# A Fourier mixing and MLP-Mixer kernel: seven-product form in three more chunks, an earlier front for batch 1, and a token relu in halves

## The chip, the cores and the metric

The kernel runs on one core of a Trainium2 chip. The metric is the device time in microseconds of one execution. The engines named below are TensorE (PE, matmuls; PEld is its weight load), VectorE (DVE), ScalarE (ACT), GpSimd (POOL) and SyncE (SP, which here only issues DMAs). Matmuls write to PSUM; DVE and ACT move their results from there to SBUF.

## What is computed

```python
def _attn_ref(x):                       # x: (8, 3008, 256) float32
    X = np.fft.fft(x, axis=1)
    X = np.fft.fft(X, axis=2)
    return X.real.astype(np.float32)

def _moe_ref(x, w_tok1, w_tok2, w_ch1, w_ch2):
    xt = x.transpose(0, 2, 1)
    h = np.maximum(xt @ w_tok1, 0.0) @ w_tok2      # tokens: 3008 -> 256 -> 3008
    u = x + h.transpose(0, 2, 1)
    h2 = np.maximum(u @ w_ch1, 0.0) @ w_ch2        # channels: 256 -> 1536 -> 256
    return (u + h2).astype(np.float32)

def reference(x, moe_w_tok1, moe_w_tok2, moe_w_ch1, moe_w_ch2):
    return _moe_ref(_attn_ref(x), moe_w_tok1, moe_w_tok2, moe_w_ch1, moe_w_ch2)
```

Eight batches go through the same steps. The output is 8 x 3008 x 256 in float32.

## The kernel before

**Stages of one batch.** A batch goes through three stages.

- *fold* (`fold`, lines 321 to 343): the loaded x (two tiles, xp and xm) is added to its mirror image into eo, in 17 steps of a generator. Batches 0 and 1 are folded on DVE, later ones on POOL.
- *front* (`front`, lines 414 to 550): a generator whose every `yield` ends one step. Eight steps make z (a small matmul pz with the fold's result, then a copy out of PSUM), twelve make w (pw, which reads all of z), then come the token product `tok1` (pt, with the carried weights hp and hq, a difference and a sum, and a relu into uu), `y` (py, a copy sqy, then yt) and `tok2` (pu, added to yt into ut, in twelve steps). For batches after the first this is 45 steps in all. `rot` fills one column of w.
- *channel MLP*: ut is cut into 6 chunks of 512 columns (the sixth has 448). `mm1` makes for each chunk the twelve products pc and evicts each with a relu into c1[:, ct]; `mm2` or `mm2_seven` multiplies c1 by wc2, adds the transposed ut (uT, brought by a DMA transpose on SP) and stores the result.

**Two forms of the second product.** `mm2` (line 668) runs four stores ks, each of 12 matmuls with 256 columns. `mm2_seven` (line 633) computes the same 2 by 2 block product with seven block products instead of eight: seven times 12 matmuls with 128 columns, with four sums of c1's quarters (`sums`, s1 to s4), partly summed weights t1w to t4w and b22 (made once on POOL by `weight_sums`) and seven small additions on DVE. `seven(b, c)` says which chunks use which form. The sixth chunk has only 448 columns; for an even batch its last 64 are put aside in tail1, and the following odd batch's sixth chunk gets them in its columns 448 to 511, so that this chunk is full.

**What sets the order.** The order on each engine is the order in which the program issues, written out by hand. The main loop (line 751) runs over batches, chunks c and ct, and slot = 12 c + ct. In each slot it issues one pc of this chunk, then a part of the previous chunk's second product (`places` and `sum_at` say at which ct, or every third ct for `mm2`), then parts of other batches: for batch 0 what is left of its own front (`own_at`), the fold of batch 1 and the copy w2r of the token weights on POOL; then, from slot `first` on, steps of the next batch's front, NFRONT of them spread evenly up to slot 71; and at the slots of `fold_at` parts of the fold after next, on POOL, each behind a small copy `hold` that ties them to a sum s4.

**Buffers.** PSUM has three buffers "mm" for pc, three "f" for the front's products and two for the second product. A new pc waits until an earlier one has been evicted. c1 has two buffers.

**Who evicts.** In `mm1` ct 0, 3, 6 and 9 are evicted by DVE and the others by ACT; where the previous chunk uses `mm2_seven`, ACT does all (`joins`). z copies of half 0 go to DVE and of half 1 to ACT for batches after the first, except for the last two small ones, which both go to DVE (line 442).

**Lines to recognize in the profile.** L90 is the helper `tt` (all two-input operations), L84 `ts`, L97 `act` (all of ACT), L101 `copy`. L424, L433 and L438 are pz, L448 and L450 pw, L517 pt, L474 py, L495 pu, L576 pc, L626 the seven products, L681 `mm2`.

Of the kernel before, what the change touches and what calls it, by code (L numbers as in the profile page):

```python
# [36 lines left out]
def kernel(  # L37
# [31 lines left out]
    def ps_f(name, dt=FP32, n=512):  # L69
        return psum.tile([P, n], dt, tag="f", name=name, bufs=3)  # L70
# [28 lines left out]
    def copy(e, out_, in_):  # L99
        if e:  # L100
            V.tensor_copy(out=out_, in_=in_)  # L101
        else:
            act(out_, in_)
# [310 lines left out]
    def front(b):  # L414
# [15 lines left out]
        for half in range(2):  # L430
            c = slice(half * P, (half + 1) * P)
            pz = ps_f("pz")
            nc.tensor.matmul(pz[:, 0:24], lhsT=eo[:, 0, c], rhs=t1n[:, half, 0, :],  # L433
                             start=True, stop=half == 0)
            if half:
                nc.tensor.matmul(pz[:, 0:24], lhsT=e128[:], rhs=cms[:],
                                 start=False, stop=True)
            nc.tensor.matmul(pz[:, 24:96], lhsT=eo[:, 16, c],  # L438
                             rhs=t1b[:].rearrange("p a k -> p (a k)"),
                             start=True, stop=True)  # L440
            zo = z[:, half, :, :].rearrange("p k (u s) -> p u k s", u=4)[:, :, :, 0]
            copy(b > 0 or half, zo, pz[:, 0:96].rearrange("p (u k) -> p u k", u=4))
            yield
        w = perb.tile([P, NG, 257], FP16, tag="w", name="w", bufs=2)
        zg = z[:].rearrange("p h (g i) s -> p h g (i s)", i=2)
# [65 lines left out]
        def tok1():  # L511
            for th in range(2):
                c = slice(th * P, (th + 1) * P)
                pt = ps_f("pt1")
                for o, n, w0, hw in ((0, 129, 0, hp), (129, 127, 130, hq)):
                    for g in range(NG):
                        nc.tensor.matmul(pt[:, o:o + n], lhsT=hw[:, g, c],  # L517
                                         rhs=w[:, g, w0:w0 + n],
                                         start=(g == 0), stop=(g == NG - 1))
                sq = perb.tile([P, P], FP32, tag="squ", name="squ", bufs=2)  # L520
                act(sq[:], pt[:, P:2 * P])
                uv = perb.tile([P, 2, P], FP32, tag="uv", name="uv", bufs=2)
                tt(uv[:, 0, :], pt[:, 0:P], sq[:], AT.subtract)
                tt(uv[:, 1, :], pt[:, 0:P], sq[:], AT.add)
                ts(uu[:, th, :, :], uv[:], 0.0, AT.max)
                yield
                if th == 0 and b > 0:
                    yield from rot()
# [25 lines left out]
                               for n in ("b22", "t1w", "t2w", "t3w", "t4w"))  # L554

    def seven(b, c):
        return c < NCH - 1 and (b > 0 or c >= 2)

    def weight_sums():
        G.tensor_copy(out=wc2[:, :, D:D + 1], in_=wc2[:, :, P:P + 1])  # L560
# [5 lines left out]
        tt(t3w[:], b22[:], b12, AT.subtract, G)  # L566
        tt(t4w[:], hi[:, :, 0:P], t2w[:], AT.subtract, G)

    def mm1(b, c, c1, ct, joins, cts=None):
        ut = state[b]["ut"]  # L570
        n = min(CW, S - CW * c)
        cts = cts or (ct,)
        pcs = [ps_mm("pc") for _ in cts]
        for h in range(2):
            for pc, ct in zip(pcs, cts):
                nc.tensor.matmul(pc[:, 0:n], lhsT=wc1[:, h, ct * P:(ct + 1) * P],  # L576
                                 rhs=ut[:, c, h, 0:n], start=(h == 0), stop=(h == 1))
# [125 lines left out]
    def take(g, n):  # L703
        for _ in range(n):
            next(g, None)
# [45 lines left out]
    for b in range(BB):  # L751
        nxt = front(b + 1) if b + 1 < BB else iter(())
        fold1 = fold(1, V) if b == 0 and BB > 1 else iter(())
        first, done = (31 if b == 0 else 0), 0
        for c in range(NCH):
            fold_at = {42: 5, 54: 5, 66: 7} if b == 0 else {30: 4, 42: 4, 54: 4, 66: 5}
            c1 = work.tile([P, NCT, CW], FP16, tag="c1", name="c1", bufs=2)
            box = {}
            joins = prev is not None and seven(*prev[0:2])
            for ct in range(NCT):  # L760
                slot = NCT * c + ct
                if b == 0 and slot < 3:
                    if slot == 0:
                        mm1(b, c, c1, ct, joins, range(3))
                else:
                    mm1(b, c, c1, ct, joins)
# [4 lines left out]
                if prev is not None and seven(*prev[0:2]):  # L771
                    if ct in places:
                        mm2_seven(*prev, places[ct], pbox)
                    if ct in sum_at:
                        sums(prev[2], pbox, sum_at[ct])
                elif prev is not None and ct % 3 == 2:
                    mm2(*prev, ct // 3, pbox)
                if slot == 1 and b == 0:
                    weight_sums()
                if b == 0:  # L780
                    take(own, own_at.get(slot, 0))
                    if 10 <= slot < 27:
                        take(fold1, 1)
                    if slot == 27 and BB > 2:
                        load_x(2)
                    if slot in (27, 29, 31, 33):
                        th, hb = (slot - 27) // 4, (slot - 27) // 2 % 2
                        G.tensor_copy(out=w2r[:, th, 32 * hb:32 * hb + 32, 0:NQ],
                                      in_=w2v[0][:, th, 32 * hb:32 * hb + 32, :])
                while done < NFRONT * (slot + 1 - first) // (71 - first):  # L790
                    take(nxt, 1)
                    done += 1
                if slot in fold_at:
                    if b + 2 < BB:
                        if slot == min(fold_at):
                            fold2 = fold(b + 2, G)
                        G.tensor_copy(out=hold[:], in_=pbox[4][:, 0, 0, 0:1])  # L797
                        take(fold2, fold_at[slot])
                    if slot == max(fold_at) and b + 3 < BB:
                        load_x(b + 3)  # L800
            if c == 5:
                if b % 2:
                    G.tensor_copy(out=c1[:, :, 448:512], in_=tail1[:])
                else:
                    G.tensor_copy(out=tail1[:], in_=c1[:, :, 384:448])
            prev, pbox, uT = (b, c, c1, uT), box, uT_next
    for s in range(4):
        mm2(*prev, s, pbox)
# [30 lines left out]
```

## Time and profile before

| what | value |
|---|---|
| time, three runs | 609.38 us median (608.84 to 610.14) |
| the profiled execution | 609.21 us |
| its span, first to last instruction | 607.4 us |
| mean granted TensorE clock | 1.000 |
| HBM read and written | 35.26 and 24.64 MB |
| mean time of pc, po, pa and pb matmuls (L576, L681, L626) | 374, 273, 219 ns (pipelined) |
| mean time of a sum s on DVE, 128x1536 | 946 to 960 ns |
| POOL idle before `hold` | 256.3 us in 23 places |

The page gives the busy time of each engine, its share of the span and the number of instructions; groups of instructions stand as line, engine, operation, output<-inputs, shape and count, with busy time, mean time of one and the idle time ahead of them. The busy shares in 40 slices show how evenly each engine is used (each slice is 15.2 us):

```profile
PE   3899899999999999999999999999999999999997
DVE  8778669765985668865887558866688657866663
ACT  8743575476655866477655666458665676546662
POOL 8541443703444045413336033460354000000000
DMA  8993912573238412392144832366123421323433
```

A digit 9 means 90% or more. TensorE is at 9 from the seventh slice on; the slices before it hold the building of the tables, batch 0's fold and front, and the first chunks. A matmul's time in the profile overlaps with that of the next one, so lengths of work on TensorE are better read from one start to the next.

### The profile page before, as it was taken

The page shows a single profiled execution, that of the slowest core. Times are in us where ns is not written, and L with a number is a line of the kernel's source. Part 1 is how long each engine was busy: PE and PEld are TensorE (multiplying, and loading weights), DVE is VectorE, ACT ScalarE, POOL GpSimd, SP SyncE. Part 2 cuts the span into 40 slices and gives each one's busy share as a digit, 9 for nine tenths or more (in the row PEclk, how much of TensorE's full clock was granted, in tenths as well). Part 3 has the DMA queues.
Part 4 walks back from the last instruction along what each step waited for, and adds up shares of the span by engine and source line. Part 5 has one row for each costly group of instructions (what it writes and reads, how often), then busy time and mean ns, then how long its engine had stood idle before and what let it go on. Part 6 is the DMA issues. An engine that isn't in the chain of part 4 may idle for free.

```text
span 607.4 us, 14835 instructions
## 1 busy us (share of the span) xinstructions
PE 588.5 (97%) x6121; PEld 420.6 (69%) x6121; DVE 438.8 (72%) x880; ACT 375.2 (62%) x725; POOL 181.8 (30%) x260
## 2 busy tenths in 40 slices
PE   3899899999999999999999999999999999999997
PEld 3656676677767776677766777667766777667776
DVE  8778669765985668865887558866688657866663
ACT  8743575476655866477655666458665676546662
POOL 8541443703444045413336033460354000000000
PEclk9999999999999999999999999999999999999999
DMA  8993912573238412392144832366123421323433
GB/s 158 210 175 52 195 36 49 109 124 77 55 71 151 113 37 61 71 192 55 45 105 86 138 76 56 75 130 124 40 55 73 95 60 37 82 73 68 98 70 88
DMA packets 83379, 55.65 MB, mean 92 GB/s; under 512 B 53746, under 2 KB 80050, under 8 KB 82546
## 3 DMA queue, kind: packets, MB, share of 16 engines
q1 hardware_dynamic: 76816, 36.82, 28.4%
q0 software_dynamic: 6176, 17.63, 15.8%
q8 instruction: 47, 0.77, 0.5%
q10 hardware_dynamic: 320, 0.26, 0.2%
q14 instruction: 20, 0.16, 0.1%
HBM read 35.26 MB, written 24.64 MB: 99 GB/s over the span
## 4 chain that ended last, share of the span: by engine, by line
PE 83%; DVE 0%; DVEq 0%; issue 0%
PE pc L576 36%; PE pa L626 16%; PE pb L626 12%; PE po L681 6%; PE pu L495 6%; PE pt L517 3%; PE py L474 1%; PE pw L448 1%; PE pz L424 1%; PE pw L450 1%; DVE s L90 0%; DVE ut L90 0%; PE pz L438 0%; DVE osb L90 0%; DVEq L834 0%; PE pz L433 0%
## 5 line engine op out<-in xcount | busy, mean ns | idle before, releaser
L97 ACT ACTIVATE c<-pc 128x512 f16<-128x512 f32 (+1 forms) x536 | 301.8, 587 | 159.1 <-PE pc L576 139.1
L576 PE MATMUL pc<-ut,wc 128*128 128x512 f16 (+1 forms) x1152 | 316.5, 374 | 0.8 <-ACT c L97 0.5
L626 PEld LDWEIGHTS <-s 128*128 128x128 f16 x1824 | 114.6, 98 | 34.2 <-DVE s L90 0.7
L576 PEld LDWEIGHTS <-wc 128*128 128x128 f16 x1152 | 97.4, 98 | 54.5 <-issue 4.8
L626 PEld LDWEIGHTS <-c 128*128 128x128 f16 x1368 | 86.3, 97 | 25.7
L797 POOL COPY hold<-s 128x1 f16<-128x1 f16 x23 | 4.3, 188 | 256.3 <-DVE s L90 256.3
L90 DVE TENSOR_TENSOR q<-pa,uT 128x256 f32<-128x256 f32 x114 | 49.2, 432 | 39.8 <-PE pa L626 39.0
L90 DVE TENSOR_TENSOR s<-c 128x1536 f16<-128x1536 f16 x76 | 73.0, 960 | 1.1 <-ACT c L97 0.9
L90 DVE TENSOR_TENSOR osb<-pb,q 128x256 f32<-128x256 f32 x114 | 48.4, 425 | 29.6 <-PE pb L626 28.2
L90 DVE TENSOR_TENSOR ut<-pu,yt 128x512 f16<-128x512 f32 (+1 forms) x96 | 63.6, 672 | 4.7 <-PE pu L495 4.7
L90 POOL TENSOR_TENSOR eo<-fa,fb 96x512 f16<-96x512 f16 (+1 forms) x48 | 54.2, 1150 | 0.0
L681 PE MATMUL po<-wc,c 128*128 128x256 f16 x432 | 53.4, 273 | 0.0
L495 PE MATMUL pu<-w2r,uu 128*128 128x512 f16 (+1 forms) x168 | 50.0, 379 | 0.9 <-DVE ut L90 0.8
L681 PEld LDWEIGHTS <-c 128*128 128x128 f16 x432 | 42.1, 97 | 12.6
L97 ACT ACTIVATE w<-pw 128x257 f16<-128x257 f32 x90 | 34.5, 384 | 8.5 <-PE pw L450 7.0
L84 DVE TENSOR_SCALAR c<-pc 128x512 f16<-128x512 f32 x40 | 27.4, 685 | 16.7 <-PE pc L576 16.6
L90 DVE TENSOR_TENSOR s<-c,s 128x1536 f16<-128x1536 f16 x38 | 36.1, 950 | 0.0
L90 DVE TENSOR_TENSOR s<-s,c 128x1536 f16<-128x1536 f16 x38 | 36.0, 946 | 0.0
L97 ACT ACTIVATE z<-pz 128x480 f16<-128x480 f32 (+1 forms) x28 | 18.2, 678 | 26.4 <-PE pz L424 26.4
L626 PE MATMUL pb<-wc,c 128*128 128x128 f16 x456 | 31.9, 219 | 0.0
L626 PE MATMUL pa<-wc,c 128*128 128x128 f16 x456 | 31.8, 219 | 0.0
L626 PE MATMUL pa<-t2w,s 128*128 128x128 f16 x456 | 31.7, 219 | 0.0
(159 smaller groups left out, 688.2 us busy)
## 6 DMA issues: line engine op xcount, KB each, us to landing
out_dram<-osb SPq DMA_DIRECT2D x83, 256.0 KB
xp<-in_x_dram POOLq DMA_DIRECT2D x14, 408.0 KB, 6.7
out_dram<-osb SPq DMA_DIRECT2D x11, 192.0 KB
uT<-ut SPq DMA_TRANSPOSE x96
w2n<-in_moe_w_tok_dram POOLq DMA_DIRECT2D x2, 752.0 KB, 11.0
w1p<-in_moe_w_tok_dram POOLq DMA_DIRECT2D x2, 384.0 KB, 8.7
wc<-in_moe_w_ch_dram POOLq DMA_DIRECT2D x1, 768.0 KB, 16.5
xp<-in_x_dram POOLq DMA_DIRECT2D x2, 272.0 KB, 6.2
```

The lines of the kernel that those rows point to most:

```text
L84: eng.tensor_scalar(out=out_, in0=in_, scalar1=s1, scalar2=None, op0=op0)
L90: eng.tensor_tensor(out=out_, in0=a, in1=b, op=op)
L97: nc.scalar.activation(out=out_, in_=in_, func=func, scale=scale, **kw)
L424: nc.tensor.matmul(pz[:, 96 * k:96 * k + 96], lhsT=eo[:, t0 + k, c], rhs=t1r, start=True, stop=True)
L448: nc.tensor.matmul(pw[:, 0:257], lhsT=zg[:, 1, g], rhs=td1[:], start=True, stop=False)
L450: nc.tensor.matmul(pw[:, 0:129], lhsT=zg[:, 0, g], rhs=td0[:], start=False, stop=True)
L474: nc.tensor.matmul(py[:, P * k:P * k + P], lhsT=w[:, 4 * c + k, o:o + P], rhs=tab[:, 4 * c + k, :], start=True, stop=True)
L495: nc.tensor.matmul(pu[:, 0:64 * nk], lhsT=uu[:, th, h, :], rhs=w2[:, th, :, 8 * c:8 * c + nk], start=(th == 0), stop=(th == 1))
L517: nc.tensor.matmul(pt[:, o:o + n], lhsT=hw[:, g, c], rhs=w[:, g, w0:w0 + n], start=(g == 0), stop=(g == NG - 1))
L576: nc.tensor.matmul(pc[:, 0:n], lhsT=wc1[:, h, ct * P:(ct + 1) * P], rhs=ut[:, c, h, 0:n], start=(h == 0), stop=(h == 1))
L626: nc.tensor.matmul(dst[:, P * a:P * a + P], lhsT=left[:, k, a, :], rhs=right[:, k, :], start=(first and k + a == 0), stop=(k == NH - 1), s ...
L681: nc.tensor.matmul(po[:, o:o + D], lhsT=c1[:, ct, ks * P:ks * P + P], rhs=wc2[:, ct, 0:D], start=(ct == 0), stop=(ct == NCT - 1))
```

## The change

It has these parts:

1. `seven` is now true also for chunk 5 of batches 1, 3 and 5. The copy of tail1 into c1 for odd batches is issued on POOL at the start of chunk 5 instead of after it. Since `joins` follows `seven`, the chunk after such a chunk has all its pc evicted by ACT.
2. Batch 1's fold on DVE: two steps in even slots and one in odd slots, in slots 9 to 20, instead of one a slot in slots 10 to 26. The load of x for batch 2 comes at slot 21 (was 27), the four w2r copies at 22, 24, 26, 28 (were 27, 29, 31, 33). The front of batch 1 begins at slot 20 (was 31). For batches after the first the front has one more, empty, step ahead of w; NFRONT is 46. The two small z copies are split between ACT (half 0) and DVE (half 1).
3. `tok1` of batch 0: the two halves of the accumulation (129 and 127 columns) go to two PSUM buffers. ACT copies the first while TensorE does the second; DVE subtracts and adds with the second half straight from PSUM, in a one-column and a 127-column piece each; the relu of the difference is on DVE, that of the sum on ACT.
4. Evictions of batch 0: chunk 0 has ct 1, 5, 7, 9, 11 on DVE, chunk 1 has none on DVE.

```diff
@@ front
             zo = z[:, half, :, :].rearrange("p k (u s) -> p u k s", u=4)[:, :, :, 0]
-            copy(b > 0 or half, zo, pz[:, 0:96].rearrange("p (u k) -> p u k", u=4))
+            copy(half, zo, pz[:, 0:96].rearrange("p (u k) -> p u k", u=4))
+            yield
+        if b:
             yield
@@ tok1
                 pt = ps_f("pt1")
+                uv = perb.tile([P, 2, P], FP32, tag="uv", name="uv", bufs=2)
                 for o, n, w0, hw in ((0, 129, 0, hp), (129, 127, 130, hq)):
+                    if b == 0 and o:
+                        sp = perb.tile([P, 129], FP32, tag="sp", name="sp", bufs=1)
+                        act(sp[:], pt[:, 0:129])
+                        pt = ps_f("pt2")
+                        tt(uv[:, 0, 0:1], sp[:, 0:1], sp[:, P:129], AT.subtract)
+                        tt(uv[:, 1, 0:1], sp[:, 0:1], sp[:, P:129], AT.add)
                     for g in range(NG):
                         nc.tensor.matmul(pt[:, o:o + n], lhsT=hw[:, g, c],
                                          rhs=w[:, g, w0:w0 + n],
                                          start=(g == 0), stop=(g == NG - 1))
+                if b == 0:
+                    tt(uv[:, 0, 1:], sp[:, 1:P], pt[:, 129:256], AT.subtract)
+                    ts(uu[:, th, 0, :], uv[:, 0, :], 0.0, AT.max)
+                    tt(uv[:, 1, 1:], sp[:, 1:P], pt[:, 129:256], AT.add)
+                    act(uu[:, th, 1, :], uv[:, 1, :], func=AFT.Relu)
+                    yield
+                    continue
                 sq = perb.tile([P, P], FP32, tag="squ", name="squ", bufs=2)
                 act(sq[:], pt[:, P:2 * P])
-                uv = perb.tile([P, 2, P], FP32, tag="uv", name="uv", bufs=2)
@@ seven, mm1
-        return c < NCH - 1 and (b > 0 or c >= 2)
+        if c == NCH - 1:
+            return b % 2 == 1 and b < BB - 1
+        return b > 0 or c >= 2
...
-    def mm1(b, c, c1, ct, joins, cts=None):
+    def mm1(b, c, c1, ct, on_v, cts=None):
...
-            if ct % 3 or joins:
+            if ct not in on_v:
                 act(c1[:, ct, 0:n], pc[:, 0:n], func=AFT.Relu)
@@ main loop
-    NFRONT = 45
+    NFRONT = 46
...
-        first, done = (31 if b == 0 else 0), 0
+        first, done = (20 if b == 0 else 0), 0
...
+            if c == 5 and b % 2:
+                G.tensor_copy(out=c1[:, :, 448:512], in_=tail1[:])
...
+            on_v = ((1, 5, 7, 9, 11), ())[c] if b == 0 and c < 2 else () if joins else (0, 3, 6, 9)
...
-                    if 10 <= slot < 27:
-                        take(fold1, 1)
-                    if slot == 27 and BB > 2:
+                    if 9 <= slot < 21:
+                        take(fold1, 2 - slot % 2)
+                    if slot == 21 and BB > 2:
                         load_x(2)
-                    if slot in (27, 29, 31, 33):
-                        th, hb = (slot - 27) // 4, (slot - 27) // 2 % 2
+                    if slot in (22, 24, 26, 28):
+                        th, hb = (slot - 22) // 4, (slot - 22) // 2 % 2
...
-            if c == 5:
-                if b % 2:
-                    G.tensor_copy(out=c1[:, :, 448:512], in_=tail1[:])
-                else:
-                    G.tensor_copy(out=tail1[:], in_=c1[:, :, 384:448])
+            if c == 5 and b % 2 == 0:
+                G.tensor_copy(out=tail1[:], in_=c1[:, :, 384:448])
```

More of the change, by code (lines that the diff above doesn't have):

```diff
@@ L763 @@
                     if slot == 0:
-                        mm1(b, c, c1, ct, joins, range(3))
+                        mm1(b, c, c1, ct, on_v, range(3))
                 else:
-                    mm1(b, c, c1, ct, joins)
+                    mm1(b, c, c1, ct, on_v)
                 if b == 0 and slot in (4, 16):
@@ L770 @@
                     uT_next = turn_u(*divmod(NCH * b + c + 1, NCH))
-                if prev is not None and seven(*prev[0:2]):
+                if joins:
                     if ct in places:
```

## The prediction

> **What bounds the kernel now.** I read the page first, then who waited for whom on TensorE, then the chain that ended last, then the timelines of TensorE (PE), VectorE (DVE), ScalarE (ACT) and GpSimd (POOL) around each TensorE gap. The page's head and its fourth part:
>
> ```profile
> span 607.4 us, 14835 instructions
> PE 588.5 (97%) x6121; PEld 420.6 (69%) x6121; DVE 438.8 (72%) x880; ACT 375.2 (62%) x725; POOL 181.8 (30%) x260
> ...
> PE 83%; DVE 0%; DVEq 0%; issue 0%
> ```
>
> The chain that ended last is matmul. From the windows view, with columns PE, PEld, DVE, ACT, POOL busy:
>
> ```profile
> 34.60:44.80 10.20, 9.69 (x51) 4.69 (x51) 8.53 (x14) 5.54 (x10) 7.33 (x6) 1.00 1.04 170
> 71.20:102.40 31.20, 28.77 (x330) 21.29 (x327) 22.37 (x44) 20.26 (x43) 12.19 (x16) 1.00 0.27 60
> 102.40:112.30 9.90, 9.90 (x93) 6.49 (x93) 9.30 (x17) 4.35 (x8) 5.18 (x7) 1.00 0.15 29
> 112.30:183.00 70.70, 70.70 (x758) 50.80 (x756) 51.69 (x98) 45.18 (x88) 25.21 (x35) 1.00 0.44 90
> ```
>
> From 102.4 us on PE is busy for the whole of each stretch. Because busy time is modelled, I also took from each step between two matmul starts the median step of its kind: after 102.4 us less than 0.1 us of excess is left up to the last matmul. So after 102.4 us only less matmul work helps; before it, only the gaps count. The gaps that the change can reach, PE's waits and timeline:
>
> ```profile
> PE pw L448 <- DVE z L101: 1.5, 1, 1.5
> PE pu L495 <- DVE ut L90: 0.8, 1, 0.8
> PE pu L495 <- DVE uv L90: 0.4, 1, 0.4
> ...
> 33.06 1.28 PE L495 MATMUL pu<-w2n,uu 128*128 128x512 f16 x4 [0.44 <-DVE uv L90]
> 39.13 1.02 PE L576 MATMUL pc<-ut,wc 128*128 128x512 f16 x4 [0.25 <-ACT c L97]
> 40.41 1.97 PE L576 MATMUL pc<-ut,wc 128*128 128x512 f16 x8 [0.25 <-ACT c L97]
> ...
> 72.83 0.28 PE L448 MATMUL pw<-td,z 128*128 128x257 f16 x1 [1.54 <-DVE z L101]
> 102.32 0.59 PE L495 MATMUL pu<-w2r,uu 128*128 128x512 f16 x2 [0.83 <-DVE ut L90]
> ```
>
> In excess over the median step they are 1.71 us at 71.1 (batch 1's z), 0.99 + 0.23 = 1.22 us at 100.1 to 102.3 (tok2 of batch 1), 0.61 + 0.07 + 0.42 = 1.09 us at 32.4 to 34.6 (token relu of batch 0), 0.42 + 0.42 + 0.08 = 0.91 us in chunk 0's first product, and 0.16 us at 44.5.
>
> **What the Trainium skill says.** "TensorE: Matmul & The Clock Gate", section "Wait — 56ns, not 53.3ns?", gives start to start N / 2.4 GHz + 2.5 ns, 55.6 ns at N = 128. The trace agrees: 56 ns for the 128-wide products, 109 to 112 for the 256-wide ones, so the second weight load of the narrow form is hidden. The same page, "Architectural detail", calls DVE and ACT strict FIFO; in the trace their instructions stand in program order, and it matters for what is put ahead of an eviction. "SBUF — State Buffer", section "Who interferes with whom", says that a DVE operation with two SBUF inputs and a GpSimd operation that reads SBUF lock each other out. The trace agrees:
>
> ```profile
> 40.59 1.52 POOL L90 TENSOR_TENSOR t3w<-b,wc 128x768 f16<-128x768 f16 x1
> 42.06 1.73 POOL L90 TENSOR_TENSOR t4w<-wc,t2w 128x768 f16<-128x768 f16 x1
> ...
> 42.31 1.76 DVE L90 TENSOR_TENSOR fb<-xm,xp 96x512 f16<-96x512 f16 x1
> 44.00 0.16 DVE L90 TENSOR_TENSOR eo<-xp,xm 96x4 f16<-96x4 f16 x1
> ```
>
> An fb that takes 0.41 us elsewhere took 1.76 here and ended when t4w had.
>
> **Part 1, seven products for chunk 5 of batches 1, 3, 5.** Before: 4 stores of 12 matmuls 256 wide, 1.33 us each in the chain (113.82, "po L681 x12"), 5.34 us. After: 7 products of 12 matmuls 128 wide, 0.67 us each (88.80 to 89.47), 4.67. The gain is 0.67 us a chunk, 2.0 us for three, where PE has no gap, so it counts in full. What is added lies on DVE and ACT: four sums of 0.87 us by pitch, 3.5 us; seven additions at 0.34 and a small copy, 2.5, for four at 0.34, 1.4; and the four c evictions at 0.60 (2.4 us) go from DVE to ACT, at 0.50 each. DVE gets 2.2 us more, ACT 2.0, in a stretch of some 11.5 us. It has room: from 183.0 to 195.5 DVE shows single idles of 1.17, 1.54 and 1.72 us, ACT of 0.98 to 1.38. The new wait is that of the third product for the second sum. From T0 = 182.80 PE has five pc (0.43), two products (0.67) and two pz (0.21) to do, up to 186.7; DVE after the old chunk's output is free at 183.9 and does s1, q, s2 by 186.1. The slack is 0.6 us; behind that product stands the whole PE queue. I take no loss; bounds 0 and 2 us a chunk (see the rival). The tail copy on POOL (0.83 us at 188.31) moves to the start of the chunk, where POOL idles 8.30 us before its hold at 178.76. SP's stores and transposes keep their order, and one store comes at the same slot as before. Nothing is charged for them.
>
> **Part 2, batch 1's fold and front.** The 17 fold steps stay on DVE; the 45 front steps that ran over 40 slots are 46 over 51. The last z copy (72.21, from a pz that PE had done by 71.2) was late because of what stood ahead of it on DVE:
>
> ```profile
> 70.60 0.95 DVE L90 TENSOR_TENSOR s<-s,c 128x1536 f16<-128x1536 f16 x1
> 71.47 0.58 DVE L101 CAST z<-pz 128x96 f16<-128x96 f32 x1
> 71.66 0.64 DVE L90 TENSOR_TENSOR osb<-pb,q 128x256 f32<-128x256 f32 x1
> 72.21 0.57 DVE L101 CAST z<-pz 128x96 f16<-128x96 f32 x1
> ```
>  Now half 0's z goes to ACT, half 1's stays, and an empty step puts at least one pc between it and pw; in the new order twelve po matmuls stand there too (0.43 × 2 + 1.33 us). I take the whole 1.71 us as gone. At 100 us DVE had been busy without a break from 97.7, with yt twice (1.27), s1 and s2 (0.94 each) ahead of the ut that frees a PSUM buffer for tok2. In the new order both yt and three tok2 steps are done before s1, so the ut of those three are not behind s2, and 9 instead of 12 remain in that chunk: DVE needs 4 × 0.87 + 7 × 0.34 + 0.3 + 9 × 0.61 = 11.7 us, PE 12 × 0.38 + 7 × 0.67 + 9 × 0.43 = 13.1. I take the 1.22 us as gone too; bounds 0 and 1.22. POOL's load of batch 2 and its w2r copies (5.58 us) come some 5 us earlier, in time that showed 14.04 us idle. SP gets batch 1's yrow moves earlier behind the same transposes; no PE wait in the trace names them.
>
> What is late next is DVE between 41 and 56 us. The fold starts a slot earlier, but POOL's weight sums begin when wc2 has landed (36.3), so fa still waits for t3w (42.1) and fb for t4w (43.8), ending 44.07 as before. New is that the eviction of c's last part now stands behind fa, fb and one eo on DVE. By pitch it runs 44.4 to 45.1, and the twelfth po matmul needs it: PE, there at 44.7, waits 0.47 us, ends the product at 45.26, where the old trace had 44.80. Then DVE does two and a half fold groups (1.45 each), output, yt, ut and z without idle up to about 56.2; PE reaches the fourth pz, which needs that z, at about 56.4. So any early time won would be lost there again.
>
> **Part 3, token relu in halves.** ACT evicts 129 columns while PE does the other 127, but on ACT the first half's relu stands before the second sp (about 31.85), then two tiny DVE operations, a subtraction, a relu and an addition follow. With 0.25 us a DVE step and 0.28 an ACT one, DVE is done at 33.0, as in the trace now. The relu of the addition (to 33.35) is now ahead of sqy on ACT, and tok2's second half waits for sqy's PSUM buffer: 33.96 instead of 33.55. First pc: h1 at 35.44 instead of 35.25, 0.19 us lost. The new split of evictions in chunk 0 (five on DVE, seven on ACT) wins it back: stalls at ct 8 (0.42) and ct 10 (0.43), the end of slot 12 at 42.16 against 42.21. So parts 2 and 3 together lose 0.46 us up to 44.8. Bounds: 1.0 won (if the sqy wait and the po wait don't come) and 1.2 lost (if each DVE step there costs 0.1 us more).
>
> **Sum.** 607.4 − 2.0 − 1.71 − 1.22 + 0.46 = 602.9 us of span. Around the span lie 609.21 − 607.4 = 1.8 us, so 604.8 us. The median of the runs (609.38) is 0.17 above the profiled one; that is within their spread (608.84 to 610.14) and I don't add it. About 0.2% (1.2 us) can be told from no change.
>
> **Rivals.**
> One stall survives or moves (0.20): the wait at 102 or the z wait comes back at another place of 56 to 75 us, because DVE is loaded there without a break. For: DVE 21.49 busy of 26.4 us from 44.8. Against: the waits' own instructions moved away from the sums. 604.8 + 1.2 = 606.0 us.
> The early loss doesn't come (0.16): the shorter relu chain and the even split win time and DVE catches up by 56 us. For: 2.17 us of gaps lie there. 604.8 − 1.0 = 603.8.
> Slower (0.05): the sums of the three new seven-product chunks queue behind POOL. Place: the first chunk of batches 2, 4, 6, where POOL still folds (181.28 to 184.55), with the lock. If s1 and s2 each wait for one POOL step of 1.15 us and the output copy for 0.3, less 0.6 of slack, each chunk loses 2.0 us, 6.0 in all: 610.8. Against: POOL is through at 184.5 and s1 isn't ready before 183.9. It decides once the loss passes 1.5 us a chunk, the 4.5 won divided by three.
> The change does less than it says (0.03, 609): the new products only replace PE work by waits of the same length.
>
> **The numbers.** Main case 0.56 at 604.8, with 604.1 to 605.5 of its own. The range 603.6 to 606.4 holds the main case and most of the first two rivals. Faster by over 0.2%: 0.92; within: 0.03; slower: 0.05.
>
> **What would show it.** Three chains of seven products where po stood (184, 327, 470 us) and no excess of PE steps after 75 us; no wait of pw for z; po's first product ending near 45.3 with a wait for DVE's c; pu's second half behind sqy near 34. A wait of the third product for s in batches 2, 4 and 6 would mean the sums are late. It is wrong if PE shows gaps over 0.3 us after 57 us.

## The result, and the profile after

| | before | after |
|---|---|---|
| median of the timed runs | 609.76 us (608.84 to 610.99) | 606.08 us (605.43 to 606.75) |
| ratio to before | | 0.9938, 95% interval 0.9916 to 0.996 |
| the profiled execution | 609.21 us | 606.75 us |
| its span | 607.4 us | 604.9 us |
| first pc starts, last matmul starts | 34.60, 603.33 us | 34.54, 600.82 us |
| from the one to the other | 568.73 us | 566.28 us |

The kernel is 3.7 us faster by the medians. The forecast was 604.8 us, with a range of 603.6 to 606.4 us. The last row leaves out the opening of the kernel, which differs from execution to execution (the last heading shows by what), and is used for all runs below; it is called the stretch. The page of the changed kernel, its head, the line of PE and the chain that ended last:

```profile
span 604.9 us, 15073 instructions
PE 586.9 (97%) x6229; PEld 420.5 (70%) x6229; DVE 441.4 (73%) x886; ACT 386.2 (64%) x749; POOL 185.2 (31%) x260
...
PE 92%; DMA 5%; DVE 1%; POOL 1%; issue 0%; DVEq 0%
```

From the po wait shown next up to the end, the chain is matmul, as before. The DMA share of 5% lies ahead of that wait: by this view it leads back over c, fb and fa on DVE to the landing of xm, a part of batch 1's x, for which fa waited 1.29 us. Whether that landing makes the wait is tested below. There are 108 more matmuls, which is 3 × (7 × 12 − 4 × 12): the three seven-product chunks. The windows view of the same kernel, columns as in the prediction:

```profile
71.20:102.40 31.20, 31.20 (x352) 22.84 (x350) 24.77 (x49) 20.51 (x41) 12.23 (x16) 1.00 0.26 57
102.40:112.30 9.90, 9.90 (x98) 6.60 (x96) 8.84 (x17) 4.39 (x9) 6.16 (x8) 1.00 0.26 58
```

Between 71.2 and 102.4 us, where PE had been idle for 2.43 us (31.20 less 28.77), there is no idle time now. But the waits of PE hold a new line, where no po waited before:

```profile
PE po L698 <- DVE c L84: 1.6, 1, 1.6
...
PE pu L497 <- DVE uv L90: 0.5, 1, 0.5
```

Its place in the timeline of the changed kernel, engine by engine (start, length, then the instruction, and in brackets the idle time ahead of it and what ended it):

```profile
43.48 1.38 PE L698 MATMUL po<-wc,c 128*128 128x256 f16 x11
46.49 0.28 PE L698 MATMUL po<-wc,c 128*128 128x256 f16 x1 [1.62 <-DVE c L84]
...
42.68 1.01 DVE L90 TENSOR_TENSOR fa<-xp,xm 96x512 f16<-96x512 f16 x1 [1.29 <-DMA xm<-in_x_dram,ix]
43.62 1.76 DVE L90 TENSOR_TENSOR fb<-xm,xp 96x512 f16<-96x512 f16 x1
45.30 0.16 DVE L90 TENSOR_TENSOR eo<-xp,xm 96x4 f16<-96x4 f16 x1
45.41 0.43 DVE L90 TENSOR_TENSOR eo<-fa,fb 96x512 f16<-96x512 f16 x1
45.75 0.68 DVE L84 TENSOR_SCALAR c<-pc 128x512 f16<-128x512 f32 x1
...
37.63 0.24 POOL L577 COPY wc<-wc 128x12 f16<-128x12 f16 x1 [9.82 <-DMA wc<-in_moe_w_ch_dram]
41.90 1.52 POOL L90 TENSOR_TENSOR t3w<-b,wc 128x768 f16<-128x768 f16 x1
43.37 1.72 POOL L90 TENSOR_TENSOR t4w<-wc,t2w 128x768 f16<-128x768 f16 x1
```

Read from the bottom: the load of wc2 landed, POOL copied its column at 37.63 and made the weight sums, the last from 43.37 to 45.09. DVE's fb overlapped with it, took 1.76 us and ended just behind it. c's last part stood behind fb and came at 45.75, and the twelfth po matmul needs it. Eleven had run. The start of the twelfth is 1.78 us later than the median step between such matmuls gives; this "excess" is how waits of PE are counted from here on.

Three waits of 0.16 us are new as well, at 125, 267 and 409 us: pa(t2w, s), the third of the seven products that run during chunk 1 of batches 1, 3 and 5. Elsewhere after 57 us no PE step is over by more than 0.1 us.

### The profile page after: what moved, and what is told of

Read it like the earlier page. It is cut to its first block, busy times and chain, and to the rows that moved or that the text cites. A ratio compares the mean times of both kernels' runs of the same rounds, so it can differ in the third digit from the quotient of the medians.

```text
span 604.9 us, 15073 instructions
## 1 busy us (share of the span) xinstructions
PE 586.9 (97%) x6229; PEld 420.5 (70%) x6229; DVE 441.4 (73%) x886; ACT 386.2 (64%) x749; POOL 185.2 (31%) x260
## 4 chain that ended last, share of the span: by engine, by line
PE 92%; DMA 5%; DVE 1%; POOL 1%; issue 0%; DVEq 0%
PE pc L593 39%; PE pa L643 18%; PE pb L643 14%; PE pu L497 7%; PE po L698 5%; DMA xm<-in_x_dram,ix 3%; PE pt L526 3%; PE py L476 2%; DMA w1m<-in_moe_w_tok_dram 2%; PE pw L450 2%; PE pz L424 1%; PE pw L452 1%; POOL xm L109 0%; DVE ix L86 0%; DVE fb L90 0%
## 5 line engine op out<-in xcount | busy, mean ns | idle before, releaser
L97 ACT ACTIVATE c<-pc 128x512 f16<-128x512 f32 (+1 forms) x551 | 311.0, 590 | 158.4 <-PE pc L593 134.2
L643 PEld LDWEIGHTS <-s 128*128 128x128 f16 x1968 | 123.4, 98 | 37.8 <-DVE s L90 1.5
L643 PEld LDWEIGHTS <-c 128*128 128x128 f16 x1476 | 93.1, 97 | 27.8
L90 DVE TENSOR_TENSOR q<-pa,uT 128x256 f32<-128x256 f32 x123 | 53.1, 432 | 45.3 <-PE pa L643 44.5
L90 DVE TENSOR_TENSOR s<-c 128x1536 f16<-128x1536 f16 x82 | 78.8, 961 | 5.5 <-ACT c L97 5.5
L90 DVE TENSOR_TENSOR osb<-pb,q 128x256 f32<-128x256 f32 x123 | 52.1, 424 | 33.4 <-PE pb L643 29.7
L698 PE MATMUL po<-wc,c 128*128 128x256 f16 x288 | 35.6, 273 | 1.6 <-DVE c L84 1.6
L698 PEld LDWEIGHTS <-c 128*128 128x128 f16 x288 | 28.0, 97 | 10.0 <-DVE c L84 1.9
L90 DVE TENSOR_TENSOR osb<-pa,uT 128x256 f32<-128x256 f32 x41 | 17.4, 425 | 23.7 <-PE pa L643 23.7
L643 PE MATMUL pa<-t4w,c 128*128 128x128 f16 x492 | 34.2, 219 | 0.0
## 6 DMA issues: line engine op xcount, KB each, us to landing
w2n<-in_moe_w_tok_dram POOLq DMA_DIRECT2D x2, 752.0 KB, 11.6
```

Source lines behind the costliest of these rows:

```text
L90: eng.tensor_tensor(out=out_, in0=a, in1=b, op=op)
L97: nc.scalar.activation(out=out_, in_=in_, func=func, scale=scale, **kw)
L643: nc.tensor.matmul(dst[:, P * a:P * a + P], lhsT=left[:, k, a, :], rhs=right[:, k, :], start=(first and k + a == 0), stop=(k == NH - 1), s ...
L698: nc.tensor.matmul(po[:, o:o + D], lhsT=c1[:, ct, ks * P:ks * P + P], rhs=wc2[:, ct, 0:D], start=(ct == 0), stop=(ct == NCT - 1))
```

## The experiments

All were timed in five rounds. The kernel before was at 610.13 to 610.24 us beside them, so the ratio says more than the microseconds. The last column of this table is the stretch from the first pc to the last matmul start in the profiled execution.

| kernel | median us | ratio, 95% interval | first pc at | pc to last |
|---|---|---|---|---|
| seven products alone | 608.52 | 0.997 (0.9957 to 0.9982) | 35.83 | 566.64 |
| c's part 11 on ACT | 606.37 | 0.9935 (0.9923 to 0.9946) | 36.17 | 564.30 |
| weight sums late | 605.5 | 0.9924 (0.991 to 0.9938) | 34.49 | 564.48 |
| old relu | 605.65 | 0.9925 (0.9912 to 0.9938) | 34.40 | 564.35 |
| changed kernel, again | 606.0 | 0.9935 (0.992 to 0.9949) | 35.54 | 564.48 |
| wc2 loaded late | 611.32 | 1.0024 (1.0015 to 1.0033) | 35.58 | 570.80 |
| small z on DVE | 605.51 | 0.9922 (0.9907 to 0.9936) | 35.70 | 563.97 |
| front from slot 31 | 607.24 | 0.9949 (0.9933 to 0.9964) | 38.11 | 565.60 |
| four edits together | 605.18 | 0.9912 (0.9898 to 0.9927) | 36.08 | 563.60 |
| changed kernel, third | 606.01 | 0.9926 (0.9912 to 0.994) | 35.79 | 564.48 |

Where the intervals overlap with the changed kernel's, as for most edits of a few tenths, the verdict rests on the trace and not on the time.

### Seven products alone

The kernel before with part 1 of the change and nothing else:

```diff
-        return c < NCH - 1 and (b > 0 or c >= 2)
+        if c == NCH - 1:
+            return b % 2 == 1 and b < BB - 1
+        return b > 0 or c >= 2
...
+            if c == 5 and b % 2:
+                G.tensor_copy(out=c1[:, :, 448:512], in_=tail1[:])
...
-            if c == 5:
-                if b % 2:
-                    G.tensor_copy(out=c1[:, :, 448:512], in_=tail1[:])
-                else:
-                    G.tensor_copy(out=tail1[:], in_=c1[:, :, 384:448])
+            if c == 5 and b % 2 == 0:
+                G.tensor_copy(out=tail1[:], in_=c1[:, :, 384:448])
```

> The kernel before with nothing but the seven-product form for chunk 5 of batches 1, 3 and 5 (and the earlier tail copy that it needs). Theory (TensorE bounds from 102 us on, sums hidden): 3 x 0.67 = 2.0 us less than the kernel before, ratio 0.9967, and no excess in TensorE's steps after 102.4 us. Rival (the sums of the new chunks queue behind POOL's fold): less than 1 us gained, and a wait of the third product for s in the first chunk of batches 2, 4 and 6.

From the first pc to the last matmul it is 2.09 us shorter than before, by time 0.3%. No product waits for a sum in the first chunks of batches 2, 4 and 6 (no step there is over by as much as 0.01 us). Both waits of batch 1's front stand as they did; PE's waits in this kernel:

```profile
PE pw L448 <- DVE z L101: 1.5, 1, 1.5
...
PE pu L495 <- DVE ut L90: 0.8, 1, 0.8
```

So part 1 is worth the 2.0 us by itself, it isn't what took these two lines away, and the slower rival (sums behind POOL) is out.

### The weight sums after the loads of batch 2

The sums leave the place where DVE folds:

```diff
-                if slot == 1 and b == 0:
-                    weight_sums()
...
                         load_x(2)
+                        weight_sums()
```

> The changed kernel with POOL's weight sums behind the load of batch 2 (so that they run from about 58 us instead of from the landing of wc2). Theory (lock between POOL's sums and DVE's fold): fa and fb take their usual 0.41 us, the twelfth po matmul waits 0.3 us or less, the span gets 1.5 to 1.8 us shorter. Rival (fa waits for the landing of xm): fa still starts after 42.6 us; then fb must be free of the lock, and the wait is between 0.3 and 0.9 us. If neither the lock nor xm is the cause, the wait stays near 1.8 us.

The timeline of DVE in this kernel:

```profile
42.41 0.42 DVE L90 TENSOR_TENSOR fa<-xp,xm 96x512 f16<-96x512 f16 x1 [1.07 <-DMA xm<-in_x_dram,ix]
42.75 0.41 DVE L90 TENSOR_TENSOR fb<-xm,xp 96x512 f16<-96x512 f16 x1
...
43.54 0.68 DVE L84 TENSOR_SCALAR c<-pc 128x512 f16<-128x512 f32 x1
```

fa and fb take 0.42 and 0.41 us without POOL beside them, c comes 1.13 us after fa starts (3.07 in the changed kernel's first profile), and no po waits. The stretch is 1.80 us shorter than in that first profile, the whole of the wait. The start of this execution was as early (first pc at 34.49), so the two compare well. It also settles two rivals. fa waited for xm here too (1.07 us), so the landing of xm by itself makes no po wait. And wc2's load was late here as well: it landed at 37.1 us, 17.4 us after its issue. By the 5.74 us that lie between POOL's copy and t4w in the first profile, sums in the old place would have had t4w start at about 42.9 us (an estimate), after fa, as in the first profile. They were not there, and neither was the wait.

### Part 11 of chunk 0 on ACT

```diff
-            on_v = ((1, 5, 7, 9, 11), ())[c] if b == 0 and c < 2 else () if joins else (0, 3, 6, 9)
+            on_v = ((1, 5, 7, 9), ())[c] if b == 0 and c < 2 else () if joins else (0, 3, 6, 9)
```

> The changed kernel with one eviction moved: ct 11 of chunk 0 of batch 0 goes to ACT instead of DVE. Theory (the 1.8 us wait of the twelfth po matmul is that eviction queued behind the fold steps that POOL's weight sums hold up): the wait falls to 0.3 us or less, the span gets 1.0 to 1.7 us shorter. Rival (DVE is simply full from 41 to 57 us): the wait comes back as waits for z or ut between 50 and 58 us, of 1 us or more, and the span changes by less than 0.5 us.

DVE's fb was blocked as in the changed kernel's first profile, yet po ran through. DVE and PE in this kernel:

```profile
42.93 0.41 DVE L90 TENSOR_TENSOR fa<-xp,xm 96x512 f16<-96x512 f16 x1
43.27 1.76 DVE L90 TENSOR_TENSOR fb<-xm,xp 96x512 f16<-96x512 f16 x1
...
44.92 1.50 PE L698 MATMUL po<-wc,c 128*128 128x256 f16 x12
```

So it is the eviction's place behind fb on DVE that passes the block on to PE. No loss followed at 50 to 58 us, so the rival (DVE is simply full there) is out. A 0.19 us wait of pc at the end of chunk 0, which stood in all three profiles of the changed kernel, went too. The time did not fall: 606.37 us. If the po wait of 1.78 us were in most executions of the changed kernel, it should have; the next two runs and the last heading bear on that.

### The changed kernel again, and a third time

No edit: the same kernel, profiled and timed on two other occasions.

> The changed kernel once more, so that it can be compared on the same chip and its wait at the twelfth po matmul seen a second time. Theory (the wait follows the landing of wc2): if wc2 lands near 36.3 us the wait is 0.3 to 0.6 us, if near 37.6 us 1.6 to 1.9 us. Rival (the wait is set by the order alone): 1.8 us whenever wc2 lands.

> The changed kernel a third time, beside the one with four edits. Theory (the wait of po's twelfth matmul is there when the weight sums on POOL, which start when wc2 lands, end later than VectorE's second group of the fold could start): if wc2 lands by 36.4 us there is no po wait, as in the second run; if it lands at 37 us or later, VectorE's second sum takes about 1.7 us and not 0.4, and po waits 1 to 2 us. Rival (the wait of 1.78 us in the first run was chance in VectorE's order, not POOL): the second sum takes 0.4 us and a po wait may come all the same. Median 605.7 to 606.4 either way.

Neither execution shows the po wait, both give 564.48 us from the first pc on, and both have the three waits of 0.16 us. So "1.8 us whenever wc2 lands" is out. The first theory had the direction and not the amount: it gave 0.3 to 0.6 us for a landing near 36.3, and with POOL's copy at 36.03 there was none. The second theory's early case came true (36.24, no wait); its late case did not occur in these two executions. DVE, POOL and PE in the second profile of the changed kernel:

```profile
42.30 1.29 DVE L90 TENSOR_TENSOR fa<-xp,xm 96x512 f16<-96x512 f16 x1
43.51 0.41 DVE L90 TENSOR_TENSOR fb<-xm,xp 96x512 f16<-96x512 f16 x1
...
44.30 0.68 DVE L84 TENSOR_SCALAR c<-pc 128x512 f16<-128x512 f32 x1
...
36.03 0.23 POOL L577 COPY wc<-wc 128x12 f16<-128x12 f16 x1 [9.23 <-DMA wc<-in_moe_w_ch_dram]
41.77 1.54 POOL L90 TENSOR_TENSOR t4w<-wc,t2w 128x768 f16<-128x768 f16 x1
...
44.48 1.50 PE L698 MATMUL po<-wc,c 128*128 128x256 f16 x12
```

wc2 landed 1.6 us earlier and PE came 1.0 us later than in the first profile. t4w had begun before fa did, so only one DVE operation was held up, and fb was free. The same order decides in every profile that has the sums in this place (three of these kernels are told below):

| profile | wc copy | t4w starts | fa starts | fb takes |
|---|---|---|---|---|
| before | 36.32 | 42.06 | 41.79 | 1.76 |
| changed, first | 37.63 | 43.37 | 42.68 | 1.76 |
| part 11 on ACT | 37.24 | 42.98 | 42.93 | 1.76 |
| seven alone | 36.58 | 42.31 | 42.88 | 0.41 |
| changed, second | 36.03 | 41.77 | 42.30 | 0.41 |
| changed, third | 36.24 | 41.98 | 42.55 | 0.41 |
| small z on DVE | 36.41 | 42.15 | 42.47 | 0.41 |
| old relu | 35.41 | 41.15 | 42.05 | 0.41 |
| front from slot 31 | 35.20 | 40.94 | 44.88 | 0.41 |

fb is blocked where t4w starts after fa, and free where it starts before. t4w starts 5.73 to 5.74 us after the copy in all of them. So the wait depends on when two things happen that the change does not order: wc2's landing and the start of fa. fa starts when DVE arrives at the fold or, as in the first profile and with the old relu (idle for 1.29 and 0.97 us), when xm has landed. Only the first of the three profiles of the changed kernel has the wait; part 11 on ACT gives a second sight of the blocked fb with a late wc2. How often the wait comes in executions without a profile can be estimated from their spans, under the last heading.

### wc2 loaded late

If the sums are what hurts, moving them so that they meet more of the fold should hurt more:

```diff
-        gdma(wc2[:, :, 0:D], dram(wc2_t, 0, [[D, P], [P * D, NCT], [1, D]]))
...
+    gdma(wc2[:, :, 0:D], dram(wc2_t, 0, [[D, P], [P * D, NCT], [1, D]]))
```

The second place is behind the loads of batch 1's x.

> The changed kernel with the load of wc2 issued after the loads of batch 1's x instead of before them. Theory (DVE's fold and the eviction behind it wait for POOL's weight sums, which start with the landing of wc2): wc2 lands later, more of the fold's steps meet a sum on POOL, and the wait of the twelfth po matmul grows to 2.5 to 5 us; the span grows by about as much as that wait. Rival (the landing of batch 1's xm sets it): xm lands earlier, fa starts before 42 us and the wait shrinks below 1 us.

It is slower than the kernel before, and 6.32 us longer from the first pc on than the changed kernel's second profile. DVE, POOL and PE of this kernel:

```profile
43.47 0.68 DVE L84 TENSOR_SCALAR c<-pc 128x512 f16<-128x512 f32 x1
...
44.73 1.72 DVE L90 TENSOR_TENSOR fa<-xp,xm 96x512 f16<-96x512 f16 x1
46.38 1.85 DVE L90 TENSOR_TENSOR fb<-xm,xp 96x512 f16<-96x512 f16 x1
48.16 1.48 DVE L90 TENSOR_TENSOR eo<-xp,xm 96x4 f16<-96x4 f16 x1
...
44.49 1.68 POOL L90 TENSOR_TENSOR t1w<-wc 128x768 f16<-128x768 f16 x1
46.25 1.70 POOL L90 TENSOR_TENSOR t2w<-b,t1w 128x768 f16<-128x768 f16 x1
47.91 1.69 POOL L90 TENSOR_TENSOR t3w<-b,wc 128x768 f16<-128x768 f16 x1
...
55.35 0.68 PE L496 MATMUL pu<-w2n,uu 128*128 128x512 f16 x2 [2.25 <-DVE yt L90]
57.07 0.56 PE L423 MATMUL pz<-t1n,eo 96*128 96x96 f16 x5 [1.04 <-DVE ut L90]
```

DVE and POOL alternate: three DVE operations in a row, even the four-column eo that takes 0.16 us elsewhere, end 0.28, 0.28 and 0.04 us after the weight sum beside them. That agrees with what the Trainium skill states in "SBUF — State Buffer", section "SBUF: two separate sides": the pair of ports that DVE and GpSimd share is an exclusive lock for the whole instruction, and the later one blocks fully. The place was another than the po wait: c's last part was evicted at 43.47, before the sums, and the twelfth po did not wait. The second fold group paid, and yt and ut behind it, for which PE waited 2.41 and 1.21 us of excess. So the theory was right that more of the fold meets a sum and that PE pays, and wrong about the twelfth po: there the rival's "below 1 us" came out, though fa did not start before 42 us (it ran from 42.34 for 0.41 us, ahead of all the sums). The other 2.7 us of the 6.32 are told under the last heading.

### The old token relu

Part 3's relu is taken back; the split of evictions stays:

```diff
-                    if b == 0 and o:
-                        sp = perb.tile([P, 129], FP32, tag="sp", name="sp", bufs=1)
-                        act(sp[:], pt[:, 0:129])
-                        pt = ps_f("pt2")
...
-                if b == 0:
-                    tt(uv[:, 0, 1:], sp[:, 1:P], pt[:, 129:256], AT.subtract)
...
```

> The changed kernel with the token relu of batch 0 as before (one PSUM buffer, ACT copies the second half). Theory (the halves gain nothing, because sqy now stands behind the second relu on ACT): the first pc's second half comes 0.1 to 0.3 us earlier than in the changed kernel (35.4 us), and the span is the same within 0.3 us, since the wait for DVE at po takes it up. Rival (the halves shorten the chain): the first pc comes later than 34.54 us by 0.3 us or more, and the span is longer by as much.

The PE excess around the relu is 0.61 + 0.07 + 0.42 = 1.09 us with the old form and 0.62 + 0.30 + 0.12 + 0.18 = 1.22 with the halves. The halves lose 0.13 us, so the rival (they shorten the chain) is out. The theory was right that they gain nothing, and wrong that a wait at po takes the difference up: there was no po wait in this execution, and its span is 602.9 us, 2.0 below the first profile of the changed kernel. By time (0.9925) the old relu can't be told from the changed kernel.

### Both small z copies on DVE from batch 2 on

The three waits of 0.16 us were put down to ACT. ACT, then DVE, of the changed kernel in chunk 1 of batch 1:

```profile
121.80 0.61 ACT L97 ACTIVATE z<-pz 128x96 f16<-128x96 f32 x1
121.93 2.55 ACT L97 ACTIVATE c<-pc 128x512 f16<-128x512 f32 x4
...
122.87 0.96 DVE L90 TENSOR_TENSOR s<-c 128x1536 f16<-128x1536 f16 x1 [1.55 <-ACT c L97]
```

DVE idled 1.55 us until the c that stands behind a small z copy, part 2's new one, had been evicted. The copies for later batches go back to DVE:

```diff
-            copy(half, zo, pz[:, 0:96].rearrange("p (u k) -> p u k", u=4))
+            copy(b > 1 or half, zo, pz[:, 0:96].rearrange("p (u k) -> p u k", u=4))
```

> The changed kernel with both small z copies on DVE for batches 2 to 7 as before; batch 1 keeps the split. Theory (the three new waits of 0.16 us of the third product, in the second chunk of batches 1, 3 and 5, come because ACT now does a small z ahead of the chunk's last eviction, which s1 waits for): the three waits go, span 0.5 us shorter. Rival (they come from the extra step that moves the front): they stay.

All three waits are gone (excess below 0.01 us at each place), and the stretch is 0.51 us shorter than the changed kernel's 564.48. In this kernel DVE makes a z copy in the gap ahead of the same sum and then waits 0.51 us in place of 1.55:

```profile
121.81 0.96 DVE L90 TENSOR_TENSOR s<-c 128x1536 f16<-128x1536 f16 x1 [0.51 <-ACT c L97]
```

Counted from DVE's own c eviction ahead of it, the sum starts after 1.81 us (120.00 to 121.81) and not after 2.24 (120.63 to 122.87), so it comes 0.43 us earlier.

### Front of batch 1 from slot 31

```diff
-        first, done = (20 if b == 0 else 0), 0
+        first, done = (31 if b == 0 else 0), 0
```

> The changed kernel with batch 1's front from slot 31 on as before; the fold in 12 slots, the empty step and the split z copies stay. Theory (the earlier start removes the wait near 102 us, the split and the empty step the wait of pw for z): the pw wait stays away or under 0.3 us, a tok2 wait near 100 us of about 1.2 us comes back, span about 1.2 us longer than the changed kernel's. Rival (the earlier start removes both): pw waits 1 us or more for z again as well.

The wait of pw for z stays away, though a pz waits for a z with 0.36 us of excess at 73.5 us. Near 103 to 108 us, waits of 0.24 + 0.41 + 0.11 = 0.76 us return, two of them ahead of pu as before. One line of each:

```profile
73.88 0.17 PE L433 MATMUL pz<-t1n,eo 96*128 96x24 f16 x1 [0.20 <-ACT z L97]
...
105.47 0.59 PE L497 MATMUL pu<-w2r,uu 128*128 128x512 f16 x2 [0.25 <-DVE ut L90]
```

Together they are 1.12 us, and the stretch is 1.12 us longer (565.60), as the theory had it. So the early start is worth 1.12 us: 0.76 of the second wait's 1.22, and 0.36 at z. It isn't what takes the wait of pw away. The split of the z copies with the empty step is the likely cause of that, but this run keeps the shorter fold and the new evictions as well, and no run takes them apart. The profiled execution was one with a late start (a pu waited 1.29 us at 35.3), so its span is not compared.

### Four edits together

Weight sums late, old relu, small z on DVE, part 11 on ACT; their diffs are above.

> Changed kernel with the four edits tried one by one: the weight sums on POOL after the loads of batch 2, the token relu whole again, both small z copies on VectorE from batch 2 on, and part 11 of the fold's first chunk on ScalarE. Theory (the waits left are those that the traces showed): no wait of po's twelfth matmul wherever wc2 lands, relu excess 1.09 and not 1.22 us, no 0.19 us wait at the end of chunk 0, no 0.16 us waits in chunk 1 of batches 1, 3 and 5; together 0.13 + 0.19 + 0.49 = 0.8 us below a run of the changed kernel without the po wait, 605.2 us, ratio to the kernel before 0.991 to 0.992. Rival (the start of the kernel, which differs by 1 us and more from execution to execution, sets what is seen): median 605.5 to 606, not to be told from the kernels with one edit each, though the trace shows the waits gone.

605.18 us against 606.01 of the changed kernel on the same chip, as the theory had it (605.2). The stretch is 563.60 us, 0.88 less; the 0.16 us waits, the 0.19 us wait and the po wait are absent, and the relu is at 1.09 us. It is the fastest of all and faster than the kernel before by 0.7 to 1.0%. That it beats the changed kernel is shown by its trace; the intervals of the two ratios (0.9898 to 0.9927, 0.9912 to 0.994) overlap. Sorted by the kind of opening (last heading), the spans no longer do: 602.3 and 602.4 against 603.1 to 604.9 us with an early opening, 603.3 to 603.8 against 604.1 to 604.6 with a late one.

## Why the prediction came out as it did

**Where the span stood.** The prediction put the span at 602.9 us; the profiled one was 604.9, with the opening equally early. Of these 2.0 us, 1.31 are the step "PE, there at 44.7, waits 0.47 us": it waited 1.78. Another 0.49 are the three 0.16 us waits, which the prediction did not have. About 0.2 remain, the size of the 0.19 us wait at the end of chunk 0. The medians (606.08, then 606.0 twice) lie inside the stated range, near its upper end, and outside the 604.1 to 605.5 of the main case. They lie beside the 606.0 us of the rival "one stall survives or moves", but not for its reason: nothing was left at 56 to 75 us or at 102.

**The step that failed: the term of 0.47 us.** The mechanism was right: fb held by t4w, c's last part behind fa, fb and one eo, po's twelfth waiting for it. The error was to fix the sums to wc2's landing of the one trace there was ("ending 44.07 as before"). wc2's copy came at 37.63 instead of 36.32, 1.31 us later, and the wait is 1.31 us longer. In the second and third profile it is zero. The prediction's bounds allowed that the po wait might not come, but their other end was 0.1 us more for each DVE step of the relu, and no later landing of wc2. A term that depends on two unordered arrivals needed a range of 0 to 1.8 us, not one value.

**Part 1: right.** 2.0 us foretold, 2.09 measured by itself. No product waited for the sums of the chunk before batches 2, 4 and 6, so the slack of 0.6 us was enough, and the slower rival did not come.

**Part 2: right for its two waits.** Neither the 1.71 us nor the 1.22 us is left at any place, and the run from slot 31 brings 0.76 us of the second back. What removes the first was not taken apart. What was missed is that a z copy moved to ACT stands in front of a c eviction in later batches too, where z had no wait to lose: 0.49 us.

**"Any early time won would be lost again": wrong.** The prediction had DVE full up to about 56.2 us and the fourth pz waiting for it. In the changed kernel's timeline DVE is through earlier and waits for PE:

```profile
54.55 0.68 DVE L90 TENSOR_TENSOR ut<-pu,yt 128x512 f16<-128x512 f32 x1
56.40 0.76 DVE L90 TENSOR_TENSOR osb<-po,uT 128x258 f32<-128x258 f32 x2 [1.18 <-PE po L698]
```

Even behind a blocked fb, 1.18 us of idle time are left there. Without the block, the 1.80 us stay won to the end (564.48 against 566.28). So the second rival, that the early loss doesn't come, has its outcome in the second and third profiles, less the 0.49 us. Its reason is not theirs: the relu in halves lost time, and the po wait is away because fb was free and PE came 1.0 and 1.25 us later.

**Part 3: right in sign.** 0.19 us lost at the relu were foretold, 0.13 measured. The stalls of chunk 0 at ct 8 and 10 are 0.42 and 0.42, as foretold; the 0.19 us wait at the end of chunk 0 was not.

**The time.** The difference foretold was 4.4 us (609.21 to 604.8). Between medians it is 3.7 in the first comparison and 4.1 to 4.2 in the later two; without the po wait the stretch is 4.25 us shorter (568.73 to 564.48). That this comes near 4.4 is partly luck: the 0.47 us that were foretold are not in it, and 0.49 + 0.19 us that were not foretold are. The absolute time stood lower than the measured one for one more reason: the sum starts from 609.21 us, a profile with an early opening, while the medians mix early and late openings (609.76 for the kernel before, later 610.1 to 610.2).

## What to carry to other kernels

When an instruction that PE needs is put behind work that shares a lock with another engine, find out what starts that other engine: if it is a DMA landing, the cost is a range between both orders of arrival, and one profile shows only one of them. Move such work to a place where nothing contends, or the needed eviction to the other engine, rather than count on the order. An operation moved between engines for one batch moves in every batch that runs the same line, so look at what it stands ahead of there too. And before medians are compared over a few tenths of a microsecond, sort the executions by their mean granted clock.

## What the runs showed of the hardware

**Half rate after a thin window.** In the run with wc2 loaded late, PE ran at half rate after its two waits. The windows of that kernel (PE, PEld, DVE, ACT, POOL busy, then the granted clock as a share of full rate), and one line of its timeline:

```profile
52.66:56.07 3.41, 1.12 (x5) 0.29 (x3) 3.41 (x11) 1.02 (x2) 0.00 (x0) 1.00 0.00 0
56.07:59.48 3.41, 2.41 (x13) 1.51 (x13) 2.50 (x9) 1.20 (x2) 1.53 (x3) 0.50 0.39 46
59.48:62.89 3.41, 3.41 (x17) 1.87 (x16) 1.81 (x4) 0.00 (x0) 3.10 (x4) 0.50 0.84 166
...
58.28 2.77 PE L697 MATMUL po<-wc,c 128*128 128x256 f16 x12
```

The clock is 0.50 from 56.07 to 62.89 us, and a chain of twelve po takes 2.77 us where it took 1.50. The steps of PE from 57.1 to 63.2 us are 2.71 us over their medians, and this is the 2.7 us that the waits leave of the loss of 6.32 (2.41 + 1.21 are the waits themselves). The Trainium skill, "TensorE: Matmul & The Clock Gate", section "What's actually happening", has the array at half rate after an idle window of some 3.4 us, which runs free of the kernel. The length agrees: the half rate lasted 6.83 us, two times 3.41. The word idle does not: PE was busy for 1.12 of the 3.41 us before the fall, and no single gap was longer than 2.4 us. So a wait of 2.4 us can cost more than itself.

**The opening is not fixed.** The three profiles of the changed kernel have the first pc at 34.54, 35.54 and 35.79 us, and wc2's copy at 37.63, 36.03 and 36.24; the two do not move together. What the late openings have in common is a half-rate window, here in the second profile, and none in the first:

```profile
15.01:18.42 3.41, 1.99 (x22) 1.01 (x18) 2.77 (x12) 3.41 (x8) 2.87 (x5) 1.00 1.12 207
18.42:21.84 3.42, 2.88 (x15) 1.94 (x15) 1.94 (x4) 1.95 (x5) 3.12 (x5) 0.50 1.18 224
...
17.80:21.22 3.42, 2.56 (x24) 1.76 (x24) 2.12 (x5) 2.47 (x7) 2.77 (x4) 1.00 1.18 216
```

All twelve profiles of this document fall into line: four without such a window have the first pc at 34.40 to 34.60 us, seven with one window at 35.54 to 36.17, and the one with two (front from slot 31) at 38.11. In the first group the clock reaches full rate at 14.1 to 14.9 us, in the others at 11.6 to 13.3, and windows of 3.41 us counted from there end at other places of the same work. What sets that start was not tried.

How much work a window needs can be worked out from these traces. For each window I add the median steps at full rate of the matmuls that start in it (216 ns for 512 columns, 112 for 256, 56 for 128). The nine windows at whose end the clock fell hold 0.19 to 0.43 of their length in such steps; the 1960 up to 585 us that kept full rate hold 0.48 or more. Of the windows at half rate, two with 0.38 and 0.41 were followed by another, and nine with 0.42 to 0.55 by full rate. This fits all twelve profiles; no run varied it on purpose.

**Executions sorted by opening.** The mean granted clock of an execution hints at its opening without a profile: in the profiles an early opening goes with 0.999 or 1.000 and a late one with 0.997 or less. Of the changed kernel's 15 timed executions, six at 0.999 or 1.000 have spans of 603.1 to 604.9 us (median 603.55) and nine at 0.996 or 0.997 have 604.1 to 604.6 (604.4). Of the kernel before in the experiments, 22 at 0.999 or 1.000 have a median span of 607.6 and 20 at 0.995 to 0.997 one of 608.7. So by these medians the change is worth 4.05 us with an early opening and 4.3 with a late one.

From the same spans comes an estimate of how often the po wait appears. The kernel with the weight sums late can't have it; its spans are 602.9 to 603.2 us with an early opening and 604.2 to 604.6 with a late one. Against these, none of the changed kernel's nine late executions shows a wait. Of the six early ones, the profiled one of 604.9 us has all of it, and the other five are longer by up to about 0.9 us, which may be part of it. This is also the likely reason why the time of the kernel with part 11 on ACT did not fall: all six of its executions opened late (0.996 or 0.997, spans 604.0 to 604.6 us), where the changed kernel shows no po wait to save.
